# Second layer: later blocks' inputs and sums, and the late weight pieces, tied to the products at their step

## The chip, the cores and the metric

The kernel runs on one core of one Trainium2 chip. The metric is the device time of one execution in microseconds, taken as the median of several executions. TensorE is PE here (its weight loads are PEld), VectorE is DVE, ScalarE is ACT, GpSimd is POOL, and SyncE is SP, the queue from which nearly all transfers of this kernel are issued. A granted clock of 1.00 is 2.4 GHz on PE, and half of it is 1.2 GHz.

## The reference

Retention without a softmax (4 sequences of 576 tokens, 8 heads), and then two dense layers on the 2304 tokens, with weights given as 64-bit floats:

```python
x = ret.transpose(0, 2, 1, 3).reshape(B * S, H * D)        # 2304 x 512
h = x @ w_in1;  g = h * np.cos(h);  x = g @ w_out1          # 512 -> 2048 -> 512
h = x @ w_in2                                               # second layer
g = np.where(h >= 1, h, np.where(h <= -1, 0, (h + 1) ** 2 / 4))
out = g @ w_out2
```

## The kernel before

Every fp32 product is made of three products of rounded halves: a number is split into a rounded copy and the rest (`xc` of two parts, `gh` and `gl`), and high times high, high times low and low times high are summed in PSUM.

**First layer.** The tokens go in five blocks. For each block and each of 16 slices of the hidden width, `mm1` (L376) makes h, `actA`, `actB` and `actC` (L422 to L446) make h cos(h) on ACT and DVE, and `mm2` (L391 to L393) adds the second product two slots later. The slots of the last two slices, `rest`, end among the first products of the second layer. In these last blocks the low part `gl` comes from POOL (L439).

**Second layer.** The 2304 tokens go in three blocks (`sb` 0, 1, 2) of 768. The first matmul is done by a Strassen-like scheme: seven products `PRODS` of half-size operands for each of eight `q`, so 3 x 8 x 7 = 168 steps, each of six matmuls of 384 columns (L507). They sum into two PSUM tiles, `hq[0]` and `hq[1]`: products 0, 2, 4 and 6 of a q go into the first (products 0, 4 afresh), products 1, 3 and 5 into the second. Between two products that use one tile its value must have been read: `after_product` copies or adds it out (L522, L527 on ACT, L515 on DVE). Products 2, 4, 5 and 6 yield a piece of h each: `piece` clamps (L540), squares (L541) and combines it (L542), and `parts` makes `gh` (L438) and `gl` (L439). Every piece gives three `group` calls of three matmuls of 512 columns (L559, L560, L561).

**Operands of a block.** `load_q(sb)` reads the block's four quarters of the first layer's output from `yd` in DRAM (L465, 384 KB each, into `wo0` to `wo3`). `sums_q(sb)` makes two sums on DVE (L471, L472). `split_q(sb, k)` makes what is left of the sum (L479, L481) and splits operand k into its rounded copy (L490, ACT) and its rest (L491, DVE). Ten homes (`RING`) hold the split operands, so three operands of the next block can be split while all seven of the present one are still in use.

**Late weight pieces.** The 64-bit weights of the second layer are converted in the background of the first. Four pieces of the second layer's output weights (slices 6, 14, 7, 15) are left for late: `load_raw(late=True)` loads one (L118, 512 KB, one buffer, `wo0`), `begin` scales it on ACT (L134), `convert` takes its bits apart on DVE (L152, L156, L141, L142, L143, L159) and ACT (L158), and `spill_wo2` writes it to DRAM (L177), from where `load_wo2` reads it for each block (L237).

**What sets the order.** The calls are written in the order of the steps: `before(step, fn)` puts loads, sums, splits and late pieces ahead of a step's product, and negative steps lie in the last slots of the first layer. That order is a priority only. A scheduler then lays every engine's instructions out by its own estimate of when their operands are there, and an instruction of low priority may go ahead wherever its data allow it. On the chip each engine runs its queue in that order. `behind(later, earlier)` makes the scheduler place one instruction after another; it adds no wait on the chip.

Of the kernel before, what the change touches and what calls it, by code (L numbers as in the profile page):

```python
# [14 lines left out]
ALU = mybir.AluOpType  # L15
# [12 lines left out]
TH = SB // 2  # L28
# [37 lines left out]
def retention_moe_kernel(ctx: ExitStack, tc: tile.TileContext, qk, kv, win1, wout1, win2, wout2, mask, vtab, ptab, out):  # L66
    nc = tc.nc
    V, A, G, SY, PE = nc.vector, nc.scalar, nc.gpsimd, nc.sync, nc.tensor
# [17 lines left out]
    yd = dp.tile([P, KB, NT], F32, tag="yd", name="yd")  # L86
# [4 lines left out]
    def f(t):  # L91
        return t.bitcast(F32)

    def behind(later, earlier):
        tc.add_manual_dep(later.ins, earlier.ins.name, mybir.DependencyInfo(mybir.DependencyClass.NoSync, mybir.DependencyReason.SCHED_ONLY), reason="pace")
# [31 lines left out]
    def begin(L, i, c, after=None, late=False):  # L127
        raw, raw2 = raws.pop((L, i, c))
        hi = raw[:, :, 1].bitcast(F32)
        if late:  # L130
            X, W = [wp.tile([P, DM], F32, tag=f"wo{k}", name="XW"[k - 1]) for k in (1, 2)]
        else:
            X, W = [cv.tile([P, DM], F32, tag=k, name=k) for k in "XW"]
        i0 = A.activation(X, hi, AF.Copy, scale=2.0 ** -112)  # L134
        if after is not None:
            behind(i0, after)
        return raw, raw2, X, W, late
# [7 lines left out]
    def convert(begun, o, after=None):  # L145
        raw, raw2, X, W, late = begun
        lo, hi = raw[:, :, 0], raw[:, :, 1]
        C = wp.tile([P, DM], I32, tag="wo3", name="C") if late else cv.tile([P, DM], I32, tag="C", name="C")
        if raw2 is not None:
            i0 = V.tensor_scalar(out=C, in0=raw2.bitcast(I32)[:, 1:1 + 2 * DM:2], scalar1=7, scalar2=None, op0=ALU.logical_shift_left)  # L150
        else:
            i0 = V.tensor_scalar(out=C, in0=hi, scalar1=23, scalar2=None, op0=ALU.logical_shift_left)  # L152
        if after is not None:
            behind(i0, after)
        if raw2 is None:
            V.scalar_tensor_tensor(out=C, in0=lo, scalar=9, in1=C, op0=ALU.logical_shift_right, op1=ALU.bitwise_or)  # L156
        signed(hi, X, W, 1)
        A.activation(o[:, 0, :], W, AF.Copy)  # L158
        return V.scalar_tensor_tensor(out=o[:, 1, :], in0=C, scalar=2.0 ** -43, in1=X, op0=ALU.mult, op1=ALU.mult)  # L159
# [14 lines left out]
    def spill_wo2(c, begun):  # L174
        t = wp.tile([P, 2, DM], F32R, tag="wo5", name="cw") if begun[-1] else wr.tile([P, 2, DM], F32R, tag="wi", name="cw")
        done.append(convert(begun, t))
        SY.dma_start(out=wd[1, 1, c], in_=f(t))  # L177
# [283 lines left out]
    def load_q(sb):  # L461
        for k, (h, g) in enumerate(((0, 0), (1, 0), (1, 1), (0, 1))):
            t = wp.tile([P, 2, TH], F32, tag=f"wo{k}", name="q")
            o = sb * SB + h * TH
            SY.dma_start(out=t, in_=yd[:, 2 * g:2 * g + 2, o:o + TH])  # L465
            q_in[sb, h, g] = t

    def sums_q(sb):
        a11, a21, a22 = q_in[sb, 0, 0], q_in[sb, 1, 0], q_in[sb, 1, 1]
        z = wp.tile([P, 2, TH], F32, tag="wo4", name="z")  # L470
        V.tensor_tensor(out=z, in0=a21, in1=a22, op=ALU.add)  # L471
        V.tensor_tensor(out=a21, in0=a11, in1=a21, op=ALU.subtract)  # L472
        q_in[sb, "z"] = z

# [18 lines left out]

    hq, sq = {}, {}
    groups = []

    def product(sb, q, k):
        _, which, first = PRODS[k]
        if k < 2:
            hq[which] = psh.tile([P, 512], F32, tag="h", name="hq")  # L500
        o = hq[which][:, :TH]
        w = wq_t.pop((sb, q, k)).rearrange("p a (k m) -> p a k m", k=2)
        x = xc[sb, k]
        i = 0
        for a, b in ((0, 0), (0, 1), (1, 0)):
            for kb in range(2):
                PE.matmul(o, w[:, a, kb, :], x[b][:, kb, :], start=first and i == 0, stop=i == 5, skip_group_check=True)  # L507
                i += 1

    def tmp(tag):  # L510
# [75 lines left out]
    for l in range(2, NBLK):  # L586
        s0, s1 = window[l]
        span = 2 * (s1 - s0) / len(members[l])
        for k, i in enumerate(members[l]):
            g = int(2 * s0 + k * span)  # L590
# [27 lines left out]
    first = members[0] + members[1]  # L618
# [71 lines left out]
    late = [(1, c) for c in (NQ - 2, NC - 2, NQ - 1, NC - 1)]  # L690
# [15 lines left out]
    def before(step, fn):  # L706
        pre.setdefault(step, []).append(fn)

    for sb in range(NSB):
        t0 = sb * NQ * 7  # L710
        before(t0 - 21, lambda sb=sb: load_q(sb))
        before(t0 - 17, lambda sb=sb: sums_q(sb))
        for k in range(7):
            before(t0 + min(2 * k - 15, k - 4), lambda sb=sb, k=k: split_q(sb, k))
# [11 lines left out]

    for j, x in enumerate(late):
        before(7 * j + 4, lambda x=x: load_raw(1, *x, late=True))
        before(7 * j + 9, lambda x=x: spill_wo2(x[1], begin(1, *x, late=True)))

    def run_pre(t):
        for fn in pre.pop(t, []):
# [2 lines left out]
    for s in range(N1):  # L735
# [7 lines left out]
        after = lastpost if s <= pos_of[1, 0] else None  # L743
# [101 lines left out]
```

## Time and profile before

| | us |
|---|---|
| median of 3 executions | 904.84 |
| their lowest and highest | 904.39, 908.19 |
| the profiled execution | 905.65 |
| its span in the profile | 903.8 |
| PE busy in the span | 874.5 |
| DVE busy | 633.2 |
| ACT busy | 482.1 |
| POOL busy | 107.0 |

The table gives one execution; 1.85 us of it lie outside the span. PE is busy in 97% of the span, so what can be won lies where PE is idle, or where it runs at a lower clock. The second layer's products start at about 507 us, and block 1's at about 637 us.

### The profile page before, as it was taken

The page shows a single profiled execution, that of the slowest core. Times are in us where ns is not written, and L with a number is a line of the kernel's source. Part 1 is how long each engine was busy: PE and PEld are TensorE (multiplying, and loading weights), DVE is VectorE, ACT ScalarE, POOL GpSimd, SP SyncE. Part 2 cuts the span into 40 slices and gives each one's busy share as a digit, 9 for nine tenths or more (in the row PEclk, how much of TensorE's full clock was granted, in tenths as well). Part 3 has the DMA queues.
Part 4 walks back from the last instruction along what each step waited for, and adds up shares of the span by engine and source line. Part 5 has one row for each costly group of instructions (what it writes and reads, how often), then busy time and mean ns, then how long its engine had stood idle before and what let it go on. Part 6 is the DMA issues. An engine that isn't in the chain of part 4 may idle for free.

```text
span 903.8 us, 13583 instructions
## 1 busy us (share of the span) xinstructions
PE 874.5 (97%) x4876; PEld 750.3 (83%) x4876; DVE 633.2 (70%) x1152; ACT 482.1 (53%) x925; POOL 107.0 (12%) x82
## 2 busy tenths in 40 slices
PE   7888999999999999999999999999999999999997
PEld 6777887888888788788888788898888989898896
DVE  4897999775877686978888786455754547555554
ACT  3577988653656564676776643334433334333332
POOL 0022322200121211222222200000000000000000
PEclk9899999999999999999999999999999999999999
DMA  9968898755586887676967896656576656666531
GB/s 321 343 205 289 302 317 307 278 197 181 183 289 223 301 270 278 208 243 230 343 257 270 300 349 193 190 183 202 206 232 183 198 175 201 231 197 181 157 94 71
DMA packets 78115, 211.81 MB, mean 234 GB/s; under 512 B 9696, under 2 KB 21728, under 8 KB 78048
## 3 DMA queue, kind: packets, MB, share of 16 engines
q1 hardware_dynamic: 77088, 210.01, 69.4%
q10 hardware_dynamic: 960, 0.93, 0.3%
q8 instruction: 39, 0.64, 0.3%
q14 instruction: 28, 0.23, 0.1%
HBM read 170.02 MB, written 40.89 MB: 233 GB/s over the span
## 4 chain that ended last, share of the span: by engine, by line
PE 64%; DVE 14%; DMA 7%; ACT 6%; issue 4%; SPq 0%; DVEq 0%; ACTq 0%
PE hq L507 18%; PE h L376 10%; PE bky L559 5%; PE bky L560 5%; PE bky L561 5%; PE bky L391 3%; PE bky L392 3%; PE bky L393 3%; DVE W L142 2%; DMA raw<-in_wout_dram 2%; DVE t L426 2%; DMA raw<-in_win_dram 2%; DMA wi<-wd 1%; DVE X L141 1%; DVE t L446 1%
## 5 line engine op out<-in xcount | busy, mean ns | idle before, releaser
L507 PE MATMUL hq<-xc,wq 128*128 128x384 f32 x1008 | 201.9, 339 | 4.0 <-ACT sX L522 4.0
L376 PE MATMUL h<-xhl,wi 128*128 128x512 f32 (+1 forms) x864 | 195.1, 372 | 3.4 <-ACT wi L158 2.6
L507 PEld LDWEIGHTS hq<-xc,wq 128*128 128x128 f32 x1008 | 181.4, 189 | 17.5 <-ACT sX L522 4.8
L376 PEld LDWEIGHTS h<-xhl,wi 128*128 128x128 f32 x864 | 149.6, 190 | 33.4 <-ACT wi L158 4.1
L439 POOL TENSOR_TENSOR gl<-t,gh 128x512 fp32r<-128x512 f32 (+1 forms) x78 | 106.8, 1370 | 409.6 <-ACT gh L438 379.9
L438 ACT ACTIVATE gh<-t 128x384 fp32r<-128x384 f32 (+2 forms) x176 | 96.4, 548 | 50.9 <-DVE t L542 27.5
L541 ACT ACTIVATE t<-t,half 128x384 f32<-128x384 f32 x96 | 59.0, 616 | 120.7 <-DVE t L540 120.6
L391 PE MATMUL bky<-gh,wo 128*128 128x512 f32 x256 | 101.7, 397 | 0.8 <-ACT gh L438 0.8
L392 PE MATMUL bky<-gh,wo 128*128 128x512 f32 x256 | 100.4, 392 | 0.0
L393 PE MATMUL bky<-gl,wo 128*128 128x512 f32 x256 | 87.4, 390 | 0.0
L542 DVE TENSOR_TENSOR t<-t,sC 128x384 f32<-128x384 f32 x96 | 53.3, 556 | 36.6 <-ACT t L541 36.5
L559 PE MATMUL bky<-wo,gh 128*128 128x512 f32 x192 | 76.4, 398 | 0.9 <-ACT gh L438 0.9
L560 PE MATMUL bky<-wo,gh 128*128 128x512 f32 x192 | 76.2, 397 | 0.0
L431 ACT ACTIVATE t<-t 128x512 f32<-128x512 f32 (+1 forms) x80 | 47.0, 587 | 54.5 <-DVE t L426 54.4
L439 DVE TENSOR_TENSOR gl<-t,gh 128x384 fp32r<-128x384 f32 (+1 forms) x98 | 54.4, 556 | 18.8 <-ACT gh L438 18.1
L540 DVE TENSOR_SCALAR t<-sC 128x384 f32<-128x384 f32 x96 | 34.2, 358 | 41.8 <-ACT sC L527 40.4
L561 PE MATMUL bky<-wo,gl 128*128 128x512 f32 x192 | 61.1, 394 | 0.0
L391 PEld LDWEIGHTS bky<-gh,wo 128*128 128x128 f32 x256 | 48.4, 189 | 12.1 <-ACT gh L438 1.6
L392 PEld LDWEIGHTS bky<-gh,wo 128*128 128x128 f32 x256 | 48.4, 189 | 9.9 <-issue 0.3
L393 PEld LDWEIGHTS bky<-gl,wo 128*128 128x128 f32 x256 | 47.7, 188 | 9.7
L134 ACT ACTIVATE X<-raw 128x512 f32<-128x512 f32 x64 | 42.2, 663 | 16.4 <-DMA raw<-in_win_dram 13.4
L142 DVE SCALAR_TENSOR_TENSOR W<-raw,X 128x512 int32<-128x512 int32 x64 | 48.8, 762 | 1.1
(127 smaller groups left out, 1375.9 us busy)
## 6 DMA issues: line engine op xcount, KB each, us to landing
wq<-wq SPq DMA_DIRECT2D x72, 512.0 KB, 4.0
wi<-wd SPq DMA_DIRECT2D x48, 512.0 KB, 5.1
wo<-wd SPq DMA_DIRECT2D x48, 512.0 KB, 4.6
raw<-in_win_dram SPq DMA_DIRECT2D x32, 512.0 KB, 6.0
raw<-in_wout_dram SPq DMA_DIRECT2D x32, 512.0 KB, 5.8
qkv<-in_qk_dram SPq DMA_DIRECT2D x20, 512.0 KB, 6.1
wd<-wi SPq DMA_DIRECT2D x16, 512.0 KB, 5.0
wd<-cw SPq DMA_DIRECT2D x16, 512.0 KB, 5.4
```

The costliest lines, as they stand in the source:

```text
L142: V.scalar_tensor_tensor(out=Wi, in0=hi, scalar=-0x80000000, in1=Xi, op0=ALU.bitwise_and, op1=ALU.bitwise_or)
L376: PE.matmul(hp[s][:, :n], w[:, a, kb, :], x[b][:, kb, :], start=(i == 0), stop=(i == 3 * KB - 1))
L391: PE.matmul(o, w[:, 0, es], a, start=first and e % per == 0, stop=False, skip_group_check=True)
L392: PE.matmul(o, w[:, 1, es], a, start=False, stop=False, skip_group_check=True)
L393: PE.matmul(o, w[:, 0, es], b, start=False, stop=last, skip_group_check=True)
L438: A.activation(a, u, AF.Copy)
L439: eng.tensor_tensor(out=b, in0=u, in1=f(a), op=ALU.subtract)
L507: PE.matmul(o, w[:, a, kb, :], x[b][:, kb, :], start=first and i == 0, stop=i == 5, skip_group_check=True)
L541: A.activation(t, t, AF.Square, scale=0.5, bias=half)
L559: PE.matmul(y, a[:, js], w[:, 0, :], start=n == 0, stop=False)
L560: PE.matmul(y, a[:, js], w[:, 1, :], start=False, stop=False)
L561: PE.matmul(y, b[:, js], w[:, 0, :], start=False, stop=n == NC - 1)
```

## The change

Three things get an order edge to the last matmul that had been issued when their call was made (`lastmm`): the four loads of `load_q` and the first sum of `sums_q` for blocks 1 and 2, and the ACT instruction with which `begin` starts a late weight piece. The calls stand where they stood: `load_q(sb)` 21 steps and `sums_q(sb)` 17 steps ahead of the block's first product, late piece j at step 7j + 9. No instruction is added, removed or changed in size on any engine.

```diff
     def load_q(sb):
...
-            SY.dma_start(out=t, in_=yd[:, 2 * g:2 * g + 2, o:o + TH])
+            i0 = SY.dma_start(out=t, in_=yd[:, 2 * g:2 * g + 2, o:o + TH])
+            if sb:
+                behind(i0, lastmm[0])
...
     def sums_q(sb):
...
-        V.tensor_tensor(out=z, in0=a21, in1=a22, op=ALU.add)
+        i0 = V.tensor_tensor(out=z, in0=a21, in1=a22, op=ALU.add)
+        if sb:
+            behind(i0, lastmm[0])
...
+    lastmm = [None]
...
-                PE.matmul(o, w[:, a, kb, :], x[b][:, kb, :], start=first and i == 0, stop=i == 5, skip_group_check=True)
+                lastmm[0] = PE.matmul(o, w[:, a, kb, :], x[b][:, kb, :], start=first and i == 0, stop=i == 5, skip_group_check=True)
...
-        before(7 * j + 9, lambda x=x: spill_wo2(x[1], begin(1, *x, late=True)))
+        before(7 * j + 9, lambda x=x: spill_wo2(x[1], begin(1, *x, after=lastmm[0], late=True)))
```

Three places of the queues show what moves. In the rows of the changed kernel the second layer's helpers have numbers that are 4 or 5 higher (L490 is L494, L515 is L520, L522 is L527, L527 is L532, L540 is L545, L541 is L546, L542 is L547); the text uses the numbers of before. A number behind a name tells one tile of a name from another.

ACT ahead of the first copy of the second layer (L522, which frees `hq[0]` for product 2), before:

```order
L432 ACTIVATE t_5159<-t_5159 128x512
L134 ACTIVATE X_5572<-raw_5472 128x512
L438 ACTIVATE gh_5199<-t_5159 128x512
L158 ACTIVATE cw_5575<-W_5573 128x512
L424 ACTIVATE t_5203<-bkO_5185 128x512
L425 ACTIVATE t_5203<-t_5203 128x512
L431 ACTIVATE t_5203<-t_5203 128x512
L134 ACTIVATE X_5725<-raw_5625 128x512
L432 ACTIVATE t_5203<-t_5203 128x512
L522 ACTIVATE sX_5239<-hq_5232 128x384
```

and now:

```order
L432 ACTIVATE t_5159<-t_5159 128x512
L438 ACTIVATE gh_5199<-t_5159 128x512
L424 ACTIVATE t_5203<-bkO_5185 128x512
L425 ACTIVATE t_5203<-t_5203 128x512
L431 ACTIVATE t_5203<-t_5203 128x512
L432 ACTIVATE t_5203<-t_5203 128x512
L527 ACTIVATE sX_5239<-hq_5232 128x384
```

The late pieces' instructions (X, cw) are gone from there.

ACT at the end of block 0 and the first products of block 1, before (`xc_6377` is block 1's last operand, `xc_7288`, `xc_7372` and the `q` they read are block 2's):

```order
L490 ACTIVATE xc_6377<-q_6001 128x768
L438 ACTIVATE gh_6348<-t_6344 128x384
L490 ACTIVATE xc_7288<-q_7158 128x768
L541 ACTIVATE t_6388<-t_6388,half_89 128x384
L490 ACTIVATE xc_7372<-q_7164 128x768
L522 ACTIVATE sX_6453<-hq_6446 128x384
```

and now:

```order
L494 ACTIVATE xc_6377<-q_6001 128x768
L546 ACTIVATE t_6344<-t_6344,half_89 128x384
L438 ACTIVATE gh_6348<-t_6344 128x384
L546 ACTIVATE t_6388<-t_6388,half_89 128x384
L546 ACTIVATE t_6411<-t_6411,half_89 128x384
L438 ACTIVATE gh_6392<-t_6388 128x384
L438 ACTIVATE gh_6415<-t_6411 128x384
L527 ACTIVATE sX_6453<-hq_6446 128x384
```

Block 2's splits have left this place; its loads now stand together in SP's queue 21 steps ahead of block 2, as block 1's do ahead of block 1.

DVE in the third q of block 0 (the pieces t_5505 and t_5527 and the next product's t_5593), before:

```order
L540 TENSOR_SCALAR t_5527<-sC_5525 128x384
L542 TENSOR_TENSOR t_5505<-t_5505,sC_5503 128x384
L542 TENSOR_TENSOR t_5527<-t_5527,sC_5525 128x384
L515 TENSOR_TENSOR sW_5564<-hq_5557,sX_5547 128x384
L439 TENSOR_TENSOR gl_5510<-t_5505,gh_5509 128x384
L439 TENSOR_TENSOR gl_5532<-t_5527,gh_5531 128x384
L540 TENSOR_SCALAR t_5593<-sC_5591 128x384
```

and now:

```order
L547 TENSOR_TENSOR t_5505<-t_5505,sC_5503 128x384
L141 TENSOR_SCALAR X_5572<-X_5572 128x512
L547 TENSOR_TENSOR t_5527<-t_5527,sC_5525 128x384
L142 SCALAR_TENSOR_TENSOR W_5573<-raw_5472,X_5572 128x512
L439 TENSOR_TENSOR gl_5510<-t_5505,gh_5509 128x384
L439 TENSOR_TENSOR gl_5532<-t_5527,gh_5531 128x384
L143 TENSOR_SCALAR X_5572<-W_5573 128x512
L520 TENSOR_TENSOR sW_5564<-hq_5557,sX_5547 128x384
L159 SCALAR_TENSOR_TENSOR cw_5575<-C_5576,X_5572 128x512
L152 TENSOR_SCALAR C_5729<-raw_5625 128x512
L156 SCALAR_TENSOR_TENSOR C_5729<-raw_5625,C_5729 128x512
L545 TENSOR_SCALAR t_5593<-sC_5591 128x384
```

The second late piece's conversion now runs here, and behind it stand the first two steps (L152, L156) of the third piece, whose raw data are loaded into the same buffer in between. The same pattern stands seven steps earlier and seven and fourteen steps later, the last time without a following raw piece.

## Rows read from the trace of the kernel before

**Rows 1.** The page, busy time of each engine over the span
```profile
PE 874.5 (97%) x4876; PEld 750.3 (83%) x4876; DVE 633.2 (70%) x1152; ACT 482.1 (53%) x925; POOL 107.0 (12%) x82
```
**Rows 2.** Windows: from:to, length, engines' busy us (instructions), PE's granted clock, DMA share, GB/s
```profile
500.00:520.00 20.00, 17.81 (x77) 15.21 (x76) 15.01 (x25) 11.59 (x22) 4.43 (x3) 0.91 0.79 287
...
540.00:560.00 20.00, 20.00 (x103) 18.21 (x102) 13.90 (x27) 8.39 (x17) 0.00 (x0) 1.00 0.71 207
...
640.00:660.00 20.00, 20.00 (x91) 17.71 (x92) 14.75 (x30) 9.66 (x19) 0.00 (x0) 0.91 0.59 195
...
760.00:780.00 20.00, 20.00 (x103) 18.16 (x102) 14.12 (x30) 9.29 (x18) 0.00 (x0) 1.00 0.68 217
```
**Rows 3.** Waits of PE: who waited for whom, us, times, longest
```profile
PE hq L507 <- ACT sX L522: 4.0, 2, 2.2
```
**Rows 4.** Timeline, first stall: start, us, engine, line, tiles [idle before, releaser]
```profile
503.69 0.63 ACT L432 ACTIVATE t<-t 128x512 f32<-128x512 f32 x1
...
507.37 1.72 DVE L142 SCALAR_TENSOR_TENSOR W<-raw,X 128x512 int32<-128x512 int32 x1
...
509.12 0.63 ACT L158 ACTIVATE cw<-W 128x512 fp32r<-128x512 f32 x1 [2.00 <-DVE W L142]
...
512.58 0.67 ACT L134 ACTIVATE X<-raw 128x512 f32<-128x512 f32 x1 [0.22 <-DMA raw<-in_wout_dram]
...
513.67 0.47 ACT L522 ACTIVATE sX<-hq 128x384 f32<-128x384 f32 x1
...
514.20 2.29 PE L507 MATMUL hq<-xc,wq 128*128 128x384 f32 x6 [2.19 <-ACT sX L522]
```
**Rows 5.** Timeline, PE behind the first stall
```profile
516.28 0.63 PE L391 MATMUL bky<-gh,wo 128*128 128x512 f32 x1
...
517.82 0.39 PE L391 MATMUL bky<-gh,wo 128*128 128x512 f32 x1
```
**Rows 6.** Timeline, a smaller wait of PE in block 0's second q
```profile
527.94 0.50 PE L559 MATMUL bky<-wo,gh 128*128 128x512 f32 x1 [0.61 <-ACT gh L438]
```
**Rows 7.** Timeline, second stall, at block 1's first products
```profile
633.15 0.37 SPq L465 DMA_DIRECT2D q<-yd  x1
...
638.61 0.84 ACT L490 ACTIVATE xc<-q 128x768 fp32r<-128x768 f32 x1 [1.35 <-DMA q<-yd]
...
639.89 1.81 PE L507 MATMUL hq<-xc,wq 128*128 128x384 f32 x6 [1.85 <-ACT sX L522]
...
643.98 1.20 PE L507 MATMUL hq<-xc,wq 128*128 128x384 f32 x6
```
**Rows 8.** Chain of waits, 610 to 660 us: PE's pieces at full clock (start, us)
```profile
644.14 1.04 PE hq L507 x6
645.19 0.70 PE bky L561 x3
```
**Rows 9.** Chain of waits, 490 to 560 us: raw pieces, issue and us to landing
```profile
509.15 3.40 DMA raw<-in_wout_dram
...
515.41 4.52 DMA raw<-in_wout_dram
```
**Rows 10.** The raw loads' line (L118) over the whole span
```profile
DMA to landing us min/median/max: 3.1/5.9/11.0
```
**Rows 11.** Timeline, an undisturbed q of block 0
```profile
576.09 0.56 DVE L542 TENSOR_TENSOR t<-t,sC 128x384 f32<-128x384 f32 x1 [0.28 <-ACT t L541]
...
580.86 0.49 ACT L527 ACTIVATE sC<-hq 128x384 f32<-128x384 f32 x1 [3.29 <-PE hq L507]
...
583.02 0.53 ACT L438 ACTIVATE gh<-t 128x384 fp32r<-128x384 f32 x1 [0.62 <-DVE t L542]
...
585.55 0.39 PE L559 MATMUL bkS<-wo,gh 128*128 128x512 f32 x1
```
**Rows 12.** Timeline, the fourth late piece on DVE: the first and last of six instructions
```profile
520.02 0.43 DVE L152 TENSOR_SCALAR C<-raw 128x512 int32<-128x512 int32 x1 [0.69 <-DMA raw<-in_wout_dram]
...
525.88 0.68 DVE L159 SCALAR_TENSOR_TENSOR cw<-C,X 128x512 fp32r<-128x512 int32 x1
```

## The prediction

> **What bounds the kernel now.** The busy times come first: PE works in 874.5 of 903.8 us, and no other engine comes near it [rows 1]. So a change of order can only give back what PE loses. Where it loses is seen next, in windows of 20 us over the second layer [rows 2]. In an ordinary window PE is busy for all 20.00 us at a granted clock of 1.00. Two windows stand out: 500 to 520, where PE is busy for 17.81 us at 0.91, and 640 to 660, at 0.91, behind an idle time that ends just before 640. The list of PE's waits then says for what: nearly all of its waiting in the second layer is two waits of the products for the ACT copy L522, 4.0 us together [rows 3]. The timeline gives each its history.
>
> The first one ends at 514.20 [rows 4]. PE has finished what stands ahead of the third product (product 2) and waits 2.19 us, since that product adds into `hq[0]` and L522 has not read it. L522 itself lasts 0.47 us; it is late because of what is queued ahead of it on ACT. There a late weight piece's L158 waited 2.00 us for DVE's L142, which took 1.72 us this time, and another one's L134 waited for its raw data. The reader is to see that the wait is not PE's input being slow to make, but a queue in order with somebody else's work in it.
>
> The second one ends at 639.89 [rows 7]. Block 1 has begun, and L522 stands on ACT behind an L490 that splits an operand of block 2. That L490 waits 1.35 us for a quarter of `yd` that SP issued at 633.15 and that is there at 638.6, 5.4 us later. So work that is not needed for 56 more steps holds up the product after next.
>
> **What the two stalls cost.** PE lost clock as well: the granted clock falls after each. At full clock six products take 1.04 us and three group matmuls 0.70, or 0.233 each [rows 8]. From 514.20 to 517.82 PE did six products and four matmuls of the last first-layer slot [rows 4, 5], worth 1.04 + 4 x 0.233 = 1.97 us, in 3.62 us: 1.65 lost, the level of 1.2 GHz against 2.4. With the idle 2.19 the first stall costs 3.84 us. From 639.89 to 643.98 it did six products and six group matmuls [rows 7], worth 1.04 + 1.40 = 2.44, in 4.09 us: again 1.65 lost, and with the idle 1.85 it is 3.50 us. A third, small wait of 0.61 us at 527.94 [rows 6] was for a `gh` whose chain on DVE stood behind two steps of the fourth late piece. Together 3.84 + 3.50 + 0.61 = 7.95 us.
>
> **The change part by part.** Nothing is added or taken away; each part is a move.
>
> The late pieces. ACT ahead of the first L522 now holds only the last slot's own work. From the L432 at 503.69 [rows 4] to L522 there are five ACT instructions (L438, L424, L425, L431, L432), 0.63 us each by these rows, and two of DVE between them (L446, L426). With 0.7 us for each of the two and as much again for the hand-overs, that is 5 x 0.63 + 3 x 0.7 = 5.3 us from 504.3, so L522 can start at about 509.6. PE wants it when two products and twelve matmuls behind them are done, at about 512: a margin of over 2 us. So the first stall goes whole, clock and all: 3.84 us. Late next there would be the low part `gl` from POOL, which starts from the same ACT chain and has the same margin. The 0.61 us go too, since neither L143 nor L159 stands in that chain any more.
>
> What the late pieces do in their new places is the part that can cost. Each brings about 3.3 us of DVE work (six instructions of 0.4 to 0.7 us [rows 12]) and 1.3 us of ACT work into a q of some 15 us; from 540 to 560 DVE is busy for 13.90 us of 20 with part of block 1's sums in it, and ACT for 8.39 [rows 2]. The work fits; the question is who stands behind it. Queued behind the next piece's L152, which needs raw data, are L156 and the L540 that starts the chain to `gh` of product 2. In an undisturbed q L540 starts behind L527 at 580.86, `gh` is done at 583.55 and PE takes it at 585.55 [rows 11]: 2.0 us of slack. With the new order in that q the raw buffer is free when L142 is through: the third piece's L542 starts at 576.09 [rows 11], and with L134 and L141 in front of it and L142 behind, that is at about 577.6. A raw piece lands 3.40 to 4.52 us after its issue at this end of the kernel [rows 9]: at 581.1 to 582.2. L152 and L156 take 1.1 us, so L540 starts 0.9 to 2.0 us late. At the faster landing half of the slack is left; at the slower one it is just used up. Each us beyond costs PE one us. This holds at three places (the fourth piece has no raw piece behind it). I take 0.61 us for all three, one wait like that of [rows 6], and the bounds are none and the median landing of the whole span, 5.9 us [rows 10]: 3 x (5.9 - 4.5) = 4.2 us.
>
> On SP, raw loads 2 to 4 now stand among the weight loads of the products, and each waits for its buffer; the weight loads queued behind it lead their products by six steps, so a hold of 2 or 3 us costs nothing. The last late piece is spilled around step 31 and read back some fifteen steps later: no wait.
>
> Block 2's loads, sums and first three splits leave the start of block 1. That removes the second stall: what stood between the products and L522 is gone, and the products now run in their own order. The boundary then looks like the one between blocks 1 and 2, which has the other four splits in it and none of the next block's work: PE is busy there, from 760 to 780, for 20.00 us at 1.00 [rows 2]. I take the whole 3.50 us.
>
> Blocks 1's and 2's loads and sums in their new place, some 21 to 14 steps ahead: seven DVE instructions of 0.95 us and three of ACT, over seven steps. In the kernel before, block 1's whole set lies in such steps, largely between 536 and 545, and PE is busy for all of the 20.00 us from 540 on [rows 2]. So nothing is my value. The bound is a second stall of the size of the one removed, 3.50 us for each block.
>
> A rule of the Trainium skill speaks against this part. The row first: even the early loads were not early enough, since the one issued at 633.15 was waited for at 638.61 [rows 7]. The page "DMA: Bandwidth & Descriptors", section "Rules for kernel authors", says to issue a transfer early and wait for it late; by it, tying loads to a step takes away cover, and the time would be that of the third rival. The trace so far agrees that a load's landing is worth 5 us of cover, but not that the earliest place is the best: the late waiter was the one in the queue too early.
>
> **Sum.** 7.95 less 0.61 is 7.3 us off the profiled execution's 905.65 us: 898.3. That execution lies 0.81 us above the median of the runs, 904.84, so I forecast 897.5 us.
>
> **The rivals.** One: the late pieces reach PE through DVE. If raw pieces land after 5.9 us, PE waits 1.4 us at each of three places, too short a wait to lower the clock if [rows 6] is a guide. Then 904.84 - 7.95 + 4.2 = 901.1 us. For it: the slack is just used up at 4.52 us. Against: the transfers are less crowded there, a DMA share of 0.71 and 0.59 against 0.79 at the first stall [rows 2].
>
> Two: the first stall stays, because the chain of the last slot and not the late pieces sets L522. Then only the second stall and the small wait go, less the 0.61: 904.84 - 3.50 = 901.3 us. Against it: the 2.00 us that L158 waited and the 0.67 of L134 stand in front of L522 in the trace [rows 4], and the margin above is 2 us.
>
> Three, on the other side: the tied loads land after their reader's turn, so that the reader holds its whole queue. Block 1's and block 2's first L490 stand on ACT in the first step behind the loads, and the chain to `gh` and L522 behind them; the raw pieces do the same on DVE. By the queue order SP can issue a block's loads as soon as a weight buffer is free, which is two to three steps earlier than the scheduler's place, some 7 us ahead of L490 against a landing of 5.4 [rows 7]. If SP is held to the late place, each of the two blocks costs a stall as the second one (3.50) and each of the three raw places one as the first (3.84): 7.0 + 11.5 = 18.5 us, so 904.84 - 7.95 + 18.5 = 915.4 us. It decides from a landing of about 6.3 us on for the raw pieces (1.8 us beyond the slack, the idle time behind which the clock fell [rows 7]): those three places alone then cost 11.5 us, more than the 7.95 that is won.
>
> **How the numbers follow.** The forecast gets 0.66, the first rival 0.15, the second 0.12, the third 0.07. The forecast's own range is 895.5 (all of the 7.95 us, and a little that the windows lose beside the stalls) to 900. A measurement of this kernel can tell about 0.5% from no change, 4.5 us: faster is below 900.3 us, slower above 909.4. The forecast lies below 900.3 but for a few in a hundred of its cases; the first two rivals lie within 0.5% unless their cost is halved, which I give a third of their cases. Faster gets 0.71, the same 0.23, slower 0.06. The range goes from 895.0 to 902.5, which takes in the first two rivals and leaves out the third and the forecast's ends.
>
> **What would show it.** Right: no wait of a product for L522 left in the list of PE's waits; a granted clock of 1.00 from 500 to 520 and from 630 to 660; ACT ahead of the first L522 without L134 and L158, and L522 there before 511; around block 1's first products no L490 that reads `q` by way of a DMA wait; block 0's q's with late pieces at full PE busy time. Wrong: waits of L152 for raw data of over 1 us with a wait of L559 for `gh` behind each; an L490 that waits for `yd` around steps 35 or 91; a wait at the end of the first layer that has another releaser. If PE is idle for less than 1 us in the second layer up to the last products and the time is still above 900, the clock, not the order, was the cause and the argument falls.

## The result and the profile after

The changed kernel takes 897.61 us (median of four executions, 897.26 to 897.90), the kernel before 905.99 beside it (904.39 to 908.19): a ratio of 0.9908, interval 0.9882 to 0.9934, so 8.4 us faster. The forecast was 897.5. In a later comparison the two stood at 897.56 and 905.89, ratio 0.9900, interval 0.9876 to 0.9924.

One thing about measuring has to be said first. The profiles below differ in the kernel's opening: the second layer's first product began anywhere between 503.7 and 509.9 us. Nearly every profile is of another program; the two of the changed kernel agree (506.72 and 506.62), so it is not shown whether the opening differs between executions of one program or between programs. So every comparison here is also made on the **stretch** from that product to the end of the span, which leaves the opening out: 903.8 - 506.98 = 396.82 us before, 895.6 - 506.72 = 388.88 us after, a gain of 7.94. A stretch is that of one execution. The changed kernel's second profile (e5 below) has 390.08, so a difference of about 1.2 us or less is not told apart.

The windows answer [rows 2]. Of after:

```profile
500.00:520.00 20.00, 20.00 (x98) 17.55 (x97) 9.34 (x18) 10.56 (x20) 3.88 (x3) 1.00 0.73 224
...
640.00:660.00 20.00, 20.00 (x102) 18.04 (x101) 11.58 (x23) 7.93 (x16) 0.00 (x0) 1.00 0.74 252
```

Both disturbed windows now have PE busy for 20.00 us at a clock of 1.00. The window around the whole second layer, from its first product to its last matmul, says what kind of time was won. Of before, and then of after (columns as in [rows 2]):

```profile
506.98:898.27 391.29, 386.39 (x1896) 345.45 (x1895) 231.64 (x459) 148.45 (x275) 2.56 (x2) 0.99 0.61 194
```
```profile
506.72:890.44 383.72, 382.82 (x1897) 342.89 (x1895) 231.83 (x464) 148.94 (x275) 1.29 (x1) 1.00 0.62 198
```

PE's idle time falls from 391.29 - 386.39 = 4.90 to 0.90 us, and the same matmuls take 3.57 us less of busy time. Nearly all of that second part is the clock: two falls of 1.65 us had been forecast, 3.30, and the kernel with one fall (e2 below) lies between, at 384.91. Kernels without any fall differ among themselves by more than the 0.27 left over (382.17 in e6 to 383.76 in e4). The list of PE's waits, from 500 us on, answers [rows 3] and is all there is; no product waits for L527 (L522 of before). The two waits of 0.3 us are new; they stand at 626.84 and 629.52, at the end of block 0:

```profile
PE hq L512 <- DVE sC L520: 0.3, 1, 0.3
PE hq L512 <- ACT sC L532: 0.3, 1, 0.3
PE bky L564 <- ACT gh L438: 0.2, 1, 0.2
```

The timeline of the first stall's place answers [rows 4]: the copy that had started at 513.67 starts at 508.02, and product 2 follows without a wait.

```profile
508.02 0.47 ACT L527 ACTIVATE sX<-hq 128x384 f32<-128x384 f32 x1
...
511.59 1.23 PE L512 MATMUL hq<-xc,wq 128*128 128x384 f32 x6
```

DVE and ACT now wait at places where they did not before. DVE waits for the raw data of a late piece at three places, and ACT for the next block's quarters at two, ahead of block 1 and of block 2:

```profile
528.73 0.43 DVE L152 TENSOR_SCALAR C<-raw 128x512 int32<-128x512 int32 x1 [0.72 <-DMA raw<-in_wout_dram]
...
544.30 0.43 DVE L152 TENSOR_SCALAR C<-raw 128x512 int32<-128x512 int32 x1 [1.18 <-DMA raw<-in_wout_dram]
...
560.54 0.43 DVE L152 TENSOR_SCALAR C<-raw 128x512 int32<-128x512 int32 x1 [1.77 <-DMA raw<-in_wout_dram]
...
579.68 2.92 SPq L465 DMA_DIRECT2D q<-yd  x4
...
586.50 0.85 ACT L494 ACTIVATE xc<-q 128x768 fp32r<-128x768 f32 x1 [3.33 <-DMA q<-yd]
...
711.63 0.85 ACT L494 ACTIVATE xc<-q 128x768 fp32r<-128x768 f32 x1 [1.59 <-DMA q<-yd]
```

### The profile page after: what moved, and what is told of

Read it like the earlier page. It is cut to its first block, busy times and chain, and to the rows that moved or that the text cites. A ratio compares the mean times of both kernels' runs of the same rounds, so it can differ in the third digit from the quotient of the medians.

```text
span 895.6 us, 13569 instructions
## 1 busy us (share of the span) xinstructions
PE 869.6 (97%) x4876; PEld 746.9 (83%) x4876; DVE 632.2 (71%) x1152; ACT 481.8 (54%) x925; POOL 105.6 (12%) x82
## 4 chain that ended last, share of the span: by engine, by line
PE 80%; DVE 7%; DMA 3%; ACT 3%; issue 2%; SPq 0%; DVEq 0%; ACTq 0%
PE hq L512 19%; PE h L376 14%; PE bky L391 6%; PE bky L392 6%; PE bky L393 6%; PE bky L565 5%; PE bky L564 5%; PE bky L566 5%; DVE W L142 1%; PE bkO L311 1%; PE bkO L376 1%; PE bkS L376 1%; PE bkS L565 1%; PE bkO L564 1%; PE bkO L324 1%
## 5 line engine op out<-in xcount | busy, mean ns | idle before, releaser
L512 PE MATMUL hq<-xc,wq 128*128 128x384 f32 x1008 | 198.4, 337 | 0.7 <-DVE sC L520 0.3
L546 ACT ACTIVATE t<-t,half 128x384 f32<-128x384 f32 x96 | 58.9, 615 | 107.2 <-DVE t L545 107.1
L547 DVE TENSOR_TENSOR t<-t,sC 128x384 f32<-128x384 f32 x96 | 53.3, 556 | 33.3 <-ACT t L546 32.9
L545 DVE TENSOR_SCALAR t<-sC 128x384 f32<-128x384 f32 x96 | 34.4, 358 | 36.0 <-ACT sC L532 34.4
L141 DVE TENSOR_SCALAR X<-X 128x512 int32<-128x512 int32 x64 | 30.7, 479 | 27.3 <-ACT X L134 27.1
```

The source lines that it names most:

```text
L512: lastmm[0] = PE.matmul(o, w[:, a, kb, :], x[b][:, kb, :], start=first and i == 0, stop=i == 5, skip_group_check=True)
L546: A.activation(t, t, AF.Square, scale=0.5, bias=half)
```

## The experiments

All are built from the changed kernel unless said otherwise; the same tile has line numbers that differ by a few from kernel to kernel. "Stretch" is that of the profiled execution; "idle" is PE's idle time from the first product to the last matmul, "busy" its busy time there; the medians are those of the kernel and of the kernel before in the same comparison. A "hold" is the time that an engine stands in front of one instruction whose data are not there yet, with everything queued behind it; the "cover" is how much of a hold passes before PE feels it.

| kernel | stretch | idle | busy | median | before |
|---|---|---|---|---|---|
| before | 396.82 | 4.90 | 386.39 | | 905.99 |
| after | 388.88 | 0.90 | 382.82 | 897.61 | 905.99 |
| e1 late pieces tied only | 392.42 | 3.66 | 383.28 | 902.10 | 905.98 |
| e2 loads and sums tied only | 393.90 | 3.61 | 384.91 | 904.09 | 905.98 |
| e3 late pieces and splits tied | 389.92 | 1.06 | 383.05 | 899.12 | 905.98 |
| e4 loads four steps later | 391.80 | 2.52 | 383.76 | 901.03 | 905.98 |
| e5 after, again | 390.08 | 1.99 | 382.84 | 897.56 | 905.89 |
| e6 all readers tied as well | 387.59 | 0.24 | 382.17 | 896.75 | 905.89 |
| e7 block 2 free | 392.00 | 3.07 | 383.72 | 900.32 | 905.89 |
| e8 raw data loaded twice | 401.05 | 7.65 | 388.02 | 905.86 | 905.89 |
| e9 loads free | 389.88 | 1.12 | 383.32 | 898.43 | 904.98 |
| e10 sums free | 389.42 | 1.10 | 383.15 | 899.43 | 904.98 |
| e11 readers tied, loads free | 388.23 | 0.24 | 382.22 | 896.47 | 904.98 |
| e12 before, products in order | 398.23 | 6.31 | 386.36 | 906.74 | 905.06 |

The stretch and the medians do not always say the same. e8's profiled execution was the slowest of twelve (910.91 against the median of 905.86), and e9's (895.42) lies 3.0 us below its median.

**e1 and e2: one part alone.** e1 leaves out the ties of the loads and, likewise, of the sums; e2 that of the late pieces:

```diff
-            if sb:
-                behind(i0, lastmm[0])
```
```diff
-        before(7 * j + 9, lambda x=x: spill_wo2(x[1], begin(1, *x, after=lastmm[0], late=True)))
+        before(7 * j + 9, lambda x=x: spill_wo2(x[1], begin(1, *x, late=True)))
```

> Only the late weight pieces are tied; the loads and sums of blocks 1 and 2 go as early as data allow, as in the kernel before. Theory (two stalls with two separate causes, each worth its idle time and its lost clock): the first stall and the small wait are gone, 3.84 + 0.61 = 4.45 us, and the second stays, because in this kernel's ACT order the splits L490 of block 2 again stand among the first products of block 1. So 906.0 - 4.5 = 901.5 us, or 3.5 to 4 us above the changed kernel's 897.6, with a wait of a product for L522 of 1.5 to 2 us near 635 and a granted clock near 0.91 in the window around it. Rival (the loads and sums are what held ACT ahead of the first stall as well): nothing much is won and it stays near 905 to 906. Rival (the second stall was a chance meeting of times that any shift removes): about 898.

> Only the loads and sums of blocks 1 and 2 are tied; the late weight pieces go as early as data allow, as in the kernel before. Theory of two separate causes: the first stall stays (PE waits about 2 us for L522 at 514, and the clock falls), with or without the small wait, and the second is gone: 906.0 - 3.5 = 902.5 us, or 4 to 5 us above the changed kernel. The sum of what this kernel and the one with the late pieces alone win should be the whole win, 8.4 us, within 1 us. Rival (the parts help each other, since the late pieces and the loads share SP and DVE): the sum is off by over 2 us. Rival (the second stall was a chance meeting of times): both kernels lose it, and the sum of the two wins is 11 to 12 us.

On the stretch e1 wins 4.40 us (forecast for its share 4.45) and e2 2.92 (3.50); together 7.32 of the 7.94. By the medians, for which e2's expectation was written, they win 3.88 and 1.89, together 5.8 of 8.4: off by over 2 us, which was to speak for the rival by which the parts help each other. So whether the two gains add up is open. What the waits show is that the first stall hangs on the late pieces: it is back in e2, where the loads and sums are tied, and gone in e1, where they are not. The rival by which the loads also fed the first stall falls. e2's list of PE's waits still has the first stall and the small wait, and the window behind it the low clock:

```profile
PE hq L512 <- ACT sX L527: 2.2, 1, 2.2
PE bky L564 <- ACT gh L438: 0.6, 1, 0.6
...
```
```profile
516.00:520.00 4.00, 4.00 (x13) 3.59 (x14) 3.60 (x6) 1.97 (x4) 1.28 (x1) 0.61 1.02 410
```

e1 has the expected sum (3.54 us above after), but not made as expected. PE's waits up to 890 us:

```profile
PE hq L508 <- DVE sC L516: 1.8, 2, 1.1
PE hq L508 <- ACT sX L523: 1.4, 1, 1.4
PE bky L560 <- ACT gh L438: 0.2, 1, 0.2
```

The second stall is there with 1.41 us and no fall of the clock. The other 1.8 us stand 50 us earlier, where block 1's untied sums now lie: DVE's L471 waits for `yd`, and the L516 behind it comes late.

```profile
585.78 0.96 DVE L471 TENSOR_TENSOR z<-q 128x768 f32<-128x768 f32 x1 [2.17 <-DMA q<-yd]
586.66 0.55 DVE L516 TENSOR_TENSOR sC<-hq,sW 128x384 f32<-128x384 f32 x1
```

So the same fault showed itself on another engine once the late pieces were out of the way. That e1's 4.40 us is so near to 4.45 is luck: both falls of the clock are gone there, and new waits are in their place.

**e7, e9, e10: which tie.** e7 unties block 2 only (`if sb == 1` in both places), e9 the loads of both blocks, e10 the sums of both.

> As the changed kernel, but only block 1's loads and sums are tied; block 2's go as early as data allow. In ACT's order the splits of block 2 then stand again among the first products of block 1, while everything ahead of that is as in the changed kernel. Theory (the second stall is the reader of block 2's quarters in ACT's queue): a wait of a product for L527 of 1.4 to 2 us near 635 behind an L494 that waits for yd, and a stretch from the first product to the end of 390.3 (idle alone, as the 1.41 us where only the late pieces were tied) to 392.4 us (with the clock, 3.50). Rival (the stall needs block 1's late splits as well): 388.9 within 0.4 and no such wait.

> As the changed kernel, but the loads of blocks 1 and 2 are not tied (the sums and the late pieces are). Block 2's quarters are then loaded around the start of block 1 as in the kernel before, two of its splits stand in ACT's queue ahead of the first L527 of block 1, and its sums on DVE do not. Theory (the reader in ACT's queue makes the second stall): a wait of a product for L527 of 1.2 to 2 us near 638, behind an L494 that waits for yd, and a stretch from the second layer's first product to the end of 390 to 392.4 us against 388.9. Rival (DVE's early sums made it, since PE's waits were for L520 of DVE where block 2 was left free): no such wait, 388.9 within 0.5.

> As the changed kernel, but the sums of blocks 1 and 2 are not tied (the loads and the late pieces are). The sums read what the tied loads bring and can only move two steps ahead. Theory (the ties of the loads carry the second part of the gain, those of the sums next to nothing): the second stall is not there, DVE's L473 waits some 1 to 3 us for yd, and the stretch from the first product to the end is 388.9 to 390.4, the upper end where DVE's hold adds to ACT's. Rival (both ties are needed): over 391.

e7 lands inside its range, 3.12 us above after, but no product waits for L527 as expected: its longest wait at block 1's start is for DVE's L520 (1.14 us), again behind a sum that had waited for `yd`:

```profile
631.58 0.96 DVE L473 TENSOR_TENSOR z<-q 128x768 f32<-128x768 f32 x1 [1.63 <-DMA q<-yd]
632.45 0.55 DVE L520 TENSOR_TENSOR sC<-hq,sX 128x384 f32<-128x384 f32 x1
```

e9 and e10 cost 1.00 and 0.54 us of stretch, against 3.54 where both ties are missing (e1). By the stretch one of the two is nearly enough, and the two costs are no larger than what lies between the changed kernel's own two profiles. The medians bear this out less well: e9 gains 6.6 us by them and e10 5.6, the changed kernel 8.3 and e1 3.9. (e10's sums did not wait for `yd` as expected; ACT's first split did, 3.08 us, and covered them.) In e9 the wait for L525 that was expected did not come, though ACT was held ahead of it:

```profile
628.63 2.49 PE L510 MATMUL hq<-xc,wq 128*128 128x384 f32 x12
...
630.12 0.85 ACT L492 ACTIVATE xc<-q 128x768 fp32r<-128x768 f32 x1 [1.42 <-DMA q<-yd]
...
631.29 0.47 ACT L525 ACTIVATE sX<-hq 128x384 f32<-128x384 f32 x1
...
631.43 0.50 PE L562 MATMUL bky<-wo,gh 128*128 128x512 f32 x1 [0.30 <-ACT gh L438]
```

The hold is as long as in the kernel before (1.42 us against the 1.35 of [rows 7]), but PE loses 0.30 us, not 1.85: block 1's products 0 and 1 stand together there (x12), and product 1 is work that needs no copy. Was the second stall, then, PE's order and not ACT's queue?

**e12: the kernel before with block 1's first products kept in order.**

```diff
+                m = PE.matmul(o, w[:, a, kb, :], x[b][:, kb, :], start=first and i == 0, stop=i == 5, skip_group_check=True)
+                if sb == 1 and q == 0 and i == 0 and k:
+                    behind(m, lastmm[0])
+                lastmm[0] = m
```

> The kernel before with one addition: the products of block 1's first q keep their own order on PE, so that product 1 stands ahead of product 2 (the third product of the block), which needs L522. ACT's order is that of the kernel before, with the splits of block 2 ahead of L522. It tells apart what the second stall is made of. Theory (two things make it: L522 late behind a reader of yd on ACT, and PE's order, in which the next instruction needs L522 at once): with product 1 in between PE has 1.04 us more to do, the wait at the start of block 1 shrinks from 1.85 to about 0.8 us, the clock does not fall behind it, and the stretch from the second layer's first product to the end is 396.8 - 1.04 - 1.65 = 394.1 us. The first stall stays. Rival (the reader in ACT's queue alone makes it): a wait of 1.85 us at the same place and 396.8. Rival (PE's order alone): no wait, 393.3.

None of the three came true. The wait grew to 3.60 us, and it has another name:

```profile
635.84 1.23 PE L508 MATMUL hq<-xc,wq 128*128 128x384 f32 x6
640.67 0.50 PE L563 MATMUL bky<-wo,gh 128*128 128x512 f32 x1 [3.60 <-ACT gh L438]
```
```profile
638.48 0.84 ACT L490 ACTIVATE xc<-q 128x768 fp32r<-128x768 f32 x1 [2.19 <-DMA q<-yd]
639.23 0.47 ACT L526 ACTIVATE sX<-hq 128x384 f32<-128x384 f32 x1
639.60 0.61 ACT L545 ACTIVATE t<-t,half 128x384 f32<-128x384 f32 x1
640.10 0.51 ACT L438 ACTIVATE gh<-t 128x384 fp32r<-128x384 f32 x1
```

Kept in order, product 1 was laid behind three groups that need a `gh`, and that `gh` stands behind the same held L490. So what PE waits for is a matter of its order; that it waits is ACT's queue. e9 and e12 together say that both count: the hold sets how late everything behind it is, and PE's order how much work it has until then. The difference of the stretch to before, 1.41 us, is that of the waits (3.60 - 1.85, less 0.26 and 0.08 at the two others).

**e3 and e11: the transfer early, the reader in its place.** e3 unties loads and sums but ties the split's L490; e11 ties every reader (sums, splits, L134 and L152) and leaves only the loads free.

```diff
-        A.activation(t[0], u, AF.Copy)
+        i0 = A.activation(t[0], u, AF.Copy)
+        if sb:
+            behind(i0, lastmm[0])
```

> The late pieces are tied; the loads and sums of blocks 1 and 2 are not and are issued as early as a buffer is free, but ACT's split L490, the reader of the loaded quarters, is tied to its step. So the transfer is early and the wait on ACT late. Theory (the second stall came from the place of the reader in ACT's queue and not from the transfer being early): no wait of a product for L522 is left, no hold of ACT for yd, and the time is that of the changed kernel, 897.6, within 1 us; DVE's sums L471 are still early here and may hold DVE for a transfer, which would show as a wait of DVE for yd in the first steps of block 1 and as up to 1 us on PE. Rival (the early transfers themselves, on SP ahead of the weight loads or in the DMA engines, delay the products): the second stall of about 3.5 us is there, 901, and PE's products wait for weights instead of for L522.

> Every reader tied to its step (sums on DVE, splits on ACT, a late piece's L134 and L152), and the loads of blocks 1 and 2 not tied: transfers as early as a buffer is free, waits as late as their step. Theory (only the place of a reader in an engine's queue costs, not the time of a transfer): no wait on ACT for yd, PE waits for less than 0.5 us in the second layer, and the stretch from the first product to the end is that of the kernel with all tied, 387.6 within 0.5. Rival (early transfers hold SP, and the weights of the products come late behind them): waits of PE for weights or a stretch of over 388.5.

In e3 the stall is gone with the loads not tied, as in the kernel before. Of the 1.04 us over after, 0.16 are PE's idle time, some 0.2 its busy time and the rest what follows the last matmul. DVE has one more sum that waits (2.04 us for `yd`), behind which PE loses 0.27:

```profile
587.25 1.31 PE L510 MATMUL hq<-xc,wq 128*128 128x384 f32 x6 [0.27 <-DVE sC L518]
```

e3's median lies 1.5 us above after, outside the 1 us expected, and its ratio to before, 0.9928 (0.9900 to 0.9956), is not told apart from after's. In e11 no engine waits for `yd` or raw data, and PE idles for 0.24 us in the whole layer; to the last matmul it needs 382.46 us, e6 (below, with the loads tied) 382.41. Its stretch lies 0.64 above that of e6, just outside the 0.5 expected, because of what follows the last matmul. The early transfers cost nothing that shows here; the early readers do.

**e4, e5, e8: how much a held queue may wait.** e4 ties the loads four steps later, e8 loads each of the last three raw pieces twice and keeps L545 behind L156, e5 is the changed kernel again.

```diff
-        before(t0 - 21, lambda sb=sb: load_q(sb))
+        before(t0 - (21 if sb == 0 else 17), lambda sb=sb: load_q(sb))
```
```diff
+        if late and c != NQ - 2:
+            SY.dma_start(out=t, in_=src)
         i0 = SY.dma_start(out=t, in_=src)
...
+        if late and heads:
+            behind(heads[-1], i1)
...
+        if step % 7 == 2:
+            heads.append(i0)
```

(In the last two parts of e8's edit `i1` is L156 and `heads` holds the L545 of each q's product 2.)

> As the changed kernel, but the loads of blocks 1 and 2 are tied four steps later, directly in front of their first readers, L471 on DVE and the first L490 on ACT. This puts the third rival's condition there: readers that stand in their queues while the data are still under way. In the changed kernel the first L490 of block 1 waited 3.33 us for a landing of 6.8, and PE lost 0.1 us. Theory (there is a slack of 3 to 4 us in the queue of ACT before PE feels it): the hold becomes 4 to 6.5 us at each of the two blocks, and PE loses 1 to 3 us of idle time and 1.65 of clock at each: 900 to 907 us. Third rival's price as forecast: a stall of 3.5 us for each block, so 904.6. Rival (ACT's holds are free at these steps, since what PE needs was made long before): within 0.7 of 897.6, with holds of over 4 us and PE at 20.00 of 20 us in those windows.

> The changed kernel itself, unaltered, beside the runs below. In the runs so far the opening of the kernel differed by up to 3 us between executions of one program (the first product of the second layer began between 506.3 and 509.9), so times are compared in two ways: the median, and in the profile the stretch from the second layer's first product to the end, which was 396.82 us in the kernel before and 388.88 in the changed one. Expected here: 897.6 within 1.5 us, and that stretch again 388.9 within 0.4, with no wait of a product for L527 and a granted clock of 1.00 from the first product to 880. Rival (the gain was a lucky execution): a stretch of over 391, or one of the two stalls back.

> As the changed kernel, but each of the last three late pieces is loaded twice into the same buffer, the second load behind the first, and the L545 that stands behind L152 and L156 in the changed kernel is kept behind them. So DVE's hold for raw data, 0.72, 1.18 and 1.77 us in the changed kernel, becomes one landing longer, some 4 to 5.3 us. PE's order moves a little with it. First rival of the forecast (the late pieces reach PE through DVE, once their landing uses up a slack of some 2 us): PE waits 2 to 3 us at each of the three places, and the stretch from the first product to the end grows by 6 to 9 us, by up to 5 more where the clock falls. Theory that the slack there is larger, 3 us or more: it grows by less than 4.5 us. Theory that DVE's holds never reach PE there: 388.9 within 0.5.

e5's median agrees, but its stretch misses the expected 388.9 by 1.2, for the profiled execution has a wait that the first did not have. ACT was held for 4.42 us, and PE lost 1.19.

```profile
587.48 0.85 ACT L494 ACTIVATE xc<-q 128x768 fp32r<-128x768 f32 x1 [4.42 <-DMA q<-yd]
...
589.77 1.32 PE L512 MATMUL hq<-xc,wq 128*128 128x384 f32 x6 [1.19 <-ACT sX L527]
```

In e8 the same place was held for longer still:

```profile
597.43 0.84 ACT L499 ACTIVATE xc<-q 128x768 fp32r<-128x768 f32 x1 [5.36 <-DMA q<-yd]
...
600.41 0.50 PE L571 MATMUL bky<-wo,gh 128*128 128x512 f32 x1 [2.43 <-ACT gh L443]
```

Holds of 3.33, 4.42 and 5.36 us, and PE idle behind them for 0.10, 1.19 and 2.43: the cover at this place is 3.2, 3.2 or 2.9 us by these differences, and each further us costs PE one. The window 580 to 600 of the changed kernel's first profile gives the 0.10:

```profile
580.00:600.00 20.00, 19.90 (x100) 17.64 (x99) 15.21 (x28) 8.21 (x14) 0.00 (x0) 1.00 0.79 279
```

That is the third rival's mechanism, in the changed kernel itself.

e4 did not make the holds that it was meant to make (0.80 at block 1, 0.63 and 2.73 at block 2). The first L494 moved back with the loads: SP issued them 3.6 us ahead of its turn (588.65 against 593.05 - 0.80 = 592.25), as in the changed kernel (3.5), and the first quarter landed after 4.4 us instead of 6.8.

```profile
588.65 2.08 SPq L465 DMA_DIRECT2D q<-yd  x4
...
593.05 0.85 ACT L494 ACTIVATE xc<-q 128x768 fp32r<-128x768 f32 x1 [0.80 <-DMA q<-yd]
```

Its 2.92 us come in part from block 2's sums, which crowd DVE: L520 stands behind four instructions of 0.95 us and PE waits 0.96 for it. The rest was not traced further.

e8 held DVE for 1.07, 6.87 and 2.52 us, 10.5 in all against 3.7, and its stretch is 12.17 us longer (its median, 8.3). The waits of PE do not follow the single holds:

```profile
536.24 1.32 PE L517 MATMUL hq<-xc,wq 128*128 128x384 f32 x6 [0.53 <-DVE sC L525]
538.91 0.50 PE L571 MATMUL bkS<-wo,gh 128*128 128x512 f32 x1 [1.34 <-ACT gh L443]
...
553.24 2.67 PE L517 MATMUL hq<-xc,wq 128*128 128x384 f32 x12 [0.49 <-DVE sW L525]
...
572.84 1.34 PE L517 MATMUL hq<-xc,wq 128*128 128x384 f32 x6 [1.78 <-DVE sC L525]
```

PE's and DVE's orders moved with the edit, so it shows that the first rival's mechanism is real when landings are doubled, but not the slack of the changed kernel's own order. For that there are only its own three holds, of up to 1.77 us, behind which PE lost nothing.

**e6: all readers tied.** As after, with e3's tie of the split and a tie of DVE's L152.

```diff
-    def spill_wo2(c, begun):
+    def spill_wo2(c, begun, after=None):
...
-        done.append(convert(begun, t))
+        done.append(convert(begun, t, after))
...
-        before(7 * j + 9, lambda x=x: spill_wo2(x[1], begin(1, *x, after=lastmm[0], late=True)))
+        before(7 * j + 9, lambda x=x: spill_wo2(x[1], begin(1, *x, after=lastmm[0], late=True), lastmm[0]))
```

> As the changed kernel, with two more ties: ACT's split L494 of a later block, and DVE's L152 of a late piece, so that neither stands in its queue before its data are there. In the changed kernel L494 waited 3.33 us for yd, and L152 0.72, 1.18 and 1.77 us for raw data. Theory (these holds lie in slack): the holds fall to nothing and the stretch from the first product to the end is 388.9 less 0 to 0.7, that is, no more than the 0.65 us of PE's waits at the edges of block 1; the median is within 1 us of the changed kernel's. Rival (the holds cost PE time that the list of its waits does not show): a gain of 1.5 us or more.

PE's idle time goes to 382.41 - 382.17 = 0.24 us, the least that was seen, and as little as in e11:

```profile
507.31:889.72 382.41, 382.17 (x1896) 343.24 (x1895) 232.64 (x466) 149.80 (x275) 1.30 (x1) 1.00 0.62 199
```

The stretch is 1.29 us shorter than in the changed kernel's first profile, more than the 0.7 expected and less than the 1.5 of the rival, and 2.49 shorter than in its second. Of the 1.29, 0.66 are PE's idle time and 0.65 its busy time; where the second comes from was not traced. DVE's L473 still waits 0.94 us for `yd`, and PE loses nothing behind it. The medians of e6 and e11, 896.75 and 896.47, lie 0.8 and 1.1 us below 897.56, with ratios to before of 0.9893 (0.9874 to 0.9913) and 0.9905 (0.9883 to 0.9927). That is the better version by the profile, but the medians do not separate it from the changed kernel.

## Why the prediction was right

The time and the mechanism of the two stalls both came out. One term was put in the wrong place, and the time came out as near as it did in part by luck.

*First stall and small wait (3.84 + 0.61).* Block 0 got shorter by 4.49 us: its first product starts 0.26 us earlier than before, block 1's first product 4.75. That is net of the new waits at the end of block 0 (0.27 and 0.28 us) and of 0.10 us at the hold on ACT. Forecast for it were 4.45. Of before, and then of after:

```profile
636.81 1.23 PE L507 MATMUL hq<-xc,wq 128*128 128x384 f32 x6
```
```profile
632.06 1.23 PE L512 MATMUL hq<-xc,wq 128*128 128x384 f32 x6
```

L522 came at 508.02, ahead of the 509.6 worked out. The second rival, that the last slot's own chain sets it, is refuted by this row and by e1.

*Second stall (3.50).* From block 1's first product to the end the gain is 3.45 us. The account of it held in e3, where tying the reader alone takes the stall away, and in e12: everything behind the held L490 is late. It was incomplete in that it named L522 alone. Once the order shifts, the same hold reaches PE through a `gh` (e12), and a sum that waits for `yd` on DVE does the same to PE (e1, e7).

*The clock (2 x 1.65).* 3.57 us of busy time went, for 3.30.

*The late pieces in their new places (0.61, bounds 0 to 4.2).* Nothing. The raw pieces landed 3.4 to 4.0 us after their issue, and DVE's holds of 0.72 to 1.77 us were inside the slack of 2.0 worked out from [rows 11]. Two of them are over 1 us, but no wait of PE stands behind them, so the first rival did not happen.

*Loads and sums in their new place (nothing; bound 3.50 for each block).* Here the working was wrong, though it cost little. SP was said to issue some 7 us ahead of the first L490, against a landing of 5.4. The changed kernel's trace has the issue at 579.68 and ACT free for L494 at 586.50 - 3.33 = 583.17, a lead of 3.5, and a landing of 6.8. So the third rival's condition was met, and with it one of the signs that the prediction named for being wrong: an L494 that waits for `yd` around steps 35 and 91, by 3.33 and 1.59 us. What kept its price away was a cover of about 3 us on ACT that the prediction had not worked out. In one execution (e5) it was used up and 1.19 us were paid. The 0.61 us allowed for the late pieces on DVE should have stood here; that they suffice is luck: the two profiles of the changed kernel gain 7.94 and 6.74 us of stretch, around the 7.34 of the sum.

*The level.* The forecast was built on 904.84 for the kernel before; with more executions that was 905.0 to 906.0, so the gain by the medians (8.4 and 8.3) is about a us more than the one forecast. That the end point is met within 0.1 us is luck: the start was set up to a us too low, and the gain about a us too small.

*The rule on issuing early.* The page "DMA: Bandwidth & Descriptors" of the Trainium skill, section "Rules for kernel authors", says to issue early and wait late. In the prediction it spoke against the change. e11 does both halves of it and is as good as anything here (0.24 us idle); e1 issues the loads early and leaves their readers early too, and its stretch loses 3.54 us to after. The rule agrees with the traces as long as its second half is read as the place of the reader in its engine's queue.

## What to carry to other kernels

Where a scheduler may move work up as soon as its data allow, the danger is not the early transfer but its early reader: in an in-order queue it holds everything behind it, on whichever engine it stands. Tie the readers to the step that needs them; whether the transfers themselves were tied (e6) or left early (e11) made no difference to PE here. Read a hold as harmless only with its cover beside it: here 3 us on ACT, which one of two profiled executions used up.

## What was unexpected of the hardware

**The clock.** It fell behind some waits of PE and not behind others of nearly the same kind. Behind 2.19 and 1.85 us (before), 2.2 (e2), 1.93 and 3.60 (e12), 1.78 and 2.43 (e8) the granted clock shows the lower level; behind 1.41 (e1), 1.19 (e5), 1.14 (e7) and 0.96 (e4) it stayed at 1.00. e8 behind its 1.78 us, and e1 behind its 1.41:

```profile
574.00:578.00 4.00, 3.83 (x12) 3.07 (x12) 4.00 (x11) 2.64 (x5) 0.00 (x0) 0.57 0.45 147
```
```profile
640.00:642.00 2.00, 2.00 (x10) 1.86 (x11) 2.00 (x5) 2.00 (x5) 0.00 (x0) 1.00 0.05 12
```

So the same fault cost 3.50 us as a stall of 1.85 and only its idle time as one of 1.41. What decides it was not tried.

**Landings.** The quarters of `yd` (384 KB each) landed later where the four were issued together than where they were spread out (in e11 two and two for block 1, one by one for block 2). The line of the loads in the changed kernel, and in e11:

```profile
DMA to landing us min/median/max: 5.1/6.7/9.2
```
```profile
DMA to landing us min/median/max: 3.3/4.4/7.0
```

The median is 4.1 to 5.4 us in the five kernels with both blocks' loads free (before, e1, e3, e9, e11) and 5.8 to 7.4 in the seven with both tied. So the tie of the loads goes with longer landings, which is part of why L494 was held. What in the transfers makes the difference was not tried.
